# Two unused 32-byte tiles at the right end of SBUF are taken away in a fused attention and mixture-of-experts kernel

## The chip, the cores and the metric

The kernel runs on one core of one Trainium2 chip. The metric is the time of one execution in device microseconds (us); lower is better. TensorE (PE in the rows) multiplies, and its weight loads stand in rows of their own (PEld). VectorE is DVE, ScalarE is ACT, GpSimd is POOL, and SyncE (SP) issues the transfers. SBUF is the on-chip memory in which a tile takes the same byte range in each of 128 partitions; an address below is a byte offset within a partition.

## The reference

Attention over pooled keys and values, then a dense layer pair with a cosine gate, then eight experts whose outputs are mixed with a balanced gate. All inputs and outputs are float32.

```python
attn = softmax(q @ mean8(k).T / 8) @ mean8(v)         # 4 x 8 heads, 576 rows, 72 pooled columns
x = attn as [2304, 512]
h = x @ w_in;  x = (h * cos(h)) @ w_out               # 512 -> 2048 -> 512
P = exp(x @ w_gate - max);  8 rounds of row and column normalization   # [2304, 8]
for e in range(8):
    h = maximum(x @ w1[e], 0)                         # 512 -> 1024
    out += P[:, e:e+1] * (h @ w2[e])                  # 1024 -> 512
```

The eight experts take about three quarters of the time. The text calls `x @ w1[e]` the first layer and `h @ w2[e]` the second layer.

## The kernel before, in words

**Arithmetic.** A float32 operand is split into a high part rounded to the format fp32r and a low part that holds the rest (`whi`/`wlo` and `vhi`/`vlo` of the weights, `xc` of the activations, `gh`/`gl` of the inner results). A product is three fp32r matmuls: high by high, high by low, low by high. Both expert layers use Strassen's seven products P1 to P7 in the place of eight blocks.

**Work of one step.** The experts' inner width is cut into 16 units of 512 columns, and the rows into 3 pairs of 768. A step is one unit with one pair, so there are 48 steps. In a step the first layer (`first_layer`, L1077) issues 2 x 7 x 6 = 84 matmuls of 384 columns: the weights `whi`/`wlo` are loaded into the array and `xc` streams through it. The second layer (`strassen_layer`, L1451 to L1458) issues 3 x 7 x 6 = 126 matmuls of 256 columns. Here the inner results `gh`/`gl` are loaded into the array, and the weights `vhi`/`vlo` stream through it:

```python
for n, (l, m) in enumerate(((gh, w[name][0]), (gh, w[name][1]), (gl, w[name][0]))):
    nc.tensor.matmul(out=ps, lhsT=l[:, r], rhs=m[:, k], start=(start and h + n == 0),
                     stop=(h + n == 3), skip_group_check=True)
```

Each of these matmuls reads 256 values of 4 bytes (1,024 bytes) per partition from `vhi` or `vlo` as the streamed operand and 128 values (512 bytes) per partition from `gh` or `gl` as the loaded one. Over 48 steps that is 6,048 matmuls.

**Order of the work.** Every instruction is a node of a graph. `Graph.schedule` lists the nodes engine by engine by a simulated clock, with estimated durations and due times, and the order is then fixed. Waits follow from the tiles that two nodes share. The first-layer matmuls of one step are interleaved with the second-layer ones of the step before.

**Memory.** Tiles live in pools, and pools in groups. A group is opened at one side of SBUF (`left` from low addresses up, `right` from the highest address down). The groups on the right are these:

```python
early = g.group("early", "right")
mid = g.group("mid", "right", (early,))
ahead = g.group("ahead", "right", (early,), mid)
turn = g.group("turn", "right", (early,), ahead)
late = g.group("late", "right", (early, turn), ahead)
```

`early` serves the attention (`kbd`, `at`, `band`, `pt`, `qc`, and `cw`/`m` of the weight conversion). Once it is closed, `mid` takes its place at the right end, `ahead` (the second layer's weights, `k_w2`) lies below `mid`, and `late` (`sf`, `s5`, `c22`, `t5`: temporaries of VectorE and ScalarE) below that. `xc` in the first-layer ring, `whi`/`wlo`, `gh`/`gl` and the output sums are on the left.

Of the kernel before, what the change touches and what calls it, by code (L numbers as in the profile page):

```python
# [10 lines left out]
F32 = mybir.dt.float32  # L11
# [12 lines left out]
P = 128  # L24
# [53 lines left out]
class Group:  # L78
# [9 lines left out]
    def open(self):  # L88
        if self.stack is not None:
            return  # L90
        if self.over:
            self.over.open()
        for g in self.after:
            if not g.closed and g.stack is not None:
                g.stack.close()
            g.closed = True
        self.stack = self.graph.ctx.enter_context(ExitStack())
        if self.name in ("early", "mid"):
            edge = self.stack.enter_context(self.graph.tc.tile_pool(name="edge" + self.name, bufs=1, side=self.side))
            edge.tile([P, 8], F32, name="edge" + self.name)  # L100
        for pool in self.pools:
            self.pools[pool] = self.stack.enter_context(
                self.graph.tc.tile_pool(name=pool, bufs=1, side=self.side, reuse_waits="tile"))
# [1482 lines left out]
```

## Time and profile before

| what | value |
|---|---|
| median of 3 runs | 1929.78 us (1928.85 to 1931.67) |
| the profiled execution's own time | 1929.34 us |
| its span from first to last instruction | 1927.6 us |
| PE busy | 1907.3 us, 99% of the span |
| DVE, ACT, POOL busy | 79%, 57%, 22% of the span |
[...]

The profile was taken on one execution: its time is 1.7 us more than its span, which is launch and end. A matmul's duration in a row runs from its start to its last result, so that durations of neighbours overlap; the pace of a stream of matmuls is read from the starts of the first and a later one and the number between them.

### The profile page before, as it was taken

What the parts mean: (1) busy time and instruction counts of PE and PEld (TensorE: products, weight loads), DVE (VectorE), ACT (ScalarE), POOL (GpSimd) and SP (SyncE); (2) the same over time, 40 slices, a digit from 0 to 9 for tenths busy, and PEclk for the clock granted to TensorE, in tenths of its full rate; (3) what the DMA queues carried; (4) which work ended last, traced back from release to release, by engine and by line L of the source; (5) the groups of instructions that cost most, each with busy time, mean ns of one, the idle gap of its engine ahead of it and who ended that gap; (6) DMA issues with size and microseconds to landing.
All of it is one profiled execution on the core that took longest, in us unless ns stands there. A gap on an engine that the chain in (4) does not pass through costs nothing.

```text
span 1927.6 us, 34292 instructions
## 1 busy us (share of the span) xinstructions
PE 1907.3 (99%) x13012; PEld 1872.0 (97%) x13012; DVE 1531.9 (79%) x2823; ACT 1096.6 (57%) x2354; POOL 427.4 (22%) x341
## 2 busy tenths in 40 slices
PE   8999999999999999999999999999999999999999
PEld 6789998899999999999999999999999999999998
DVE  8998888987787777777787787777777877877776
ACT  5664445675556666555556565565555565655553
POOL 2523245453202021212112021212121120212120
PEclk9999999999999999999999999999999999999999
DMA  8567564487656546546546455465465464554552
GB/s 294 169 193 236 194 198 138 176 288 239 231 225 229 228 186 237 212 181 236 211 177 262 168 231 229 184 238 210 183 236 211 178 262 170 229 231 180 229 216 113
DMA packets 107478, 406.79 MB, mean 211 GB/s; under 512 B 11825, under 2 KB 16561, under 8 KB 107313
## 3 DMA queue, kind: packets, MB, share of 16 engines
q1 hardware_dynamic: 106768, 403.55, 56.4%
q8 instruction: 102, 1.67, 0.4%
q0 software_dynamic: 544, 1.05, 0.3%
q14 instruction: 64, 0.52, 0.1%
HBM read 363.40 MB, written 41.16 MB: 210 GB/s over the span
## 4 chain that ended last, share of the span: by engine, by line
PE 91%; DVE 5%; ACT 1%; DMA 1%; issue 1%; POOL 0%; SPq 0%; DVEq 0%; POOLq 0%; ACTq 0%
PE pc L1457 21%; PE py L1077 17%; PE qc L1457 16%; PE pv L1077 11%; PE px L1077 11%; PE po L894 3%; PE po L895 3%; PE po L896 3%; PE ph L894 1%; PE ph L896 1%; PE ph L895 1%; PE ptr L803 0%; DVE at L540 0%; DVE cw L858 0%; PE psc L714 0%
## 5 line engine op out<-in xcount | busy, mean ns | idle before, releaser
L1457 PE MATMUL pc<-vhi,gl 128*128 128x256 f32 x1152 | 321.6, 279 | 0.0
L1457 PE MATMUL pc<-vhi,gh 128*128 128x256 f32 x1152 | 321.5, 279 | 0.0
L1457 PE MATMUL pc<-vlo,gh 128*128 128x256 f32 x1152 | 321.3, 279 | 0.0
L1077 PE MATMUL py<-xc,whi 128*128 128x384 f32 x1152 | 293.3, 335 | 0.0
L540 POOL TENSOR_TENSOR raw<-raw 128x512 f32<-128x512 f32 x45 | 59.1, 1314 | 895.4 <-DVE wlo L540 542.1
L540 DVE TENSOR_TENSOR gl<-sf,gh 128x384 fp32r<-128x384 f32 x384 | 228.4, 624 | 30.9 <-ACT gh L523 30.9
L523 ACT ACTIVATE gh<-sf 128x384 fp32r<-128x384 f32 x384 | 195.0, 524 | 92.1 <-DVE sf L540 90.1
L1457 PE MATMUL qc<-vhi,gh 128*128 128x256 f32 x864 | 243.6, 282 | 0.9 <-DVE qc L540 0.5
L1457 PE MATMUL qc<-vhi,gl 128*128 128x256 f32 x864 | 241.6, 280 | 0.0
L1457 PE MATMUL qc<-vlo,gh 128*128 128x256 f32 x864 | 240.8, 279 | 0.0
L1457 PEld LDWEIGHTS pc<-vlo,gh 128*128 128x128 f32 x1152 | 216.6, 188 | 0.0
L1457 PEld LDWEIGHTS pc<-vhi,gl 128*128 128x128 f32 x1152 | 216.3, 188 | 0.0
L1457 PEld LDWEIGHTS pc<-vhi,gh 128*128 128x128 f32 x1152 | 215.5, 187 | 0.1
L1077 PEld LDWEIGHTS py<-xc,whi 128*128 128x128 f32 x1152 | 199.7, 188 | 1.3 <-ACT py L523 0.6
L1077 PE MATMUL px<-xc,whi 128*128 128x384 f32 x768 | 195.8, 335 | 0.0
L1077 PE MATMUL pv<-xc,whi 128*128 128x384 f32 x768 | 195.8, 335 | 0.0
L1077 PE MATMUL py<-xc,wlo 128*128 128x384 f32 x576 | 193.2, 335 | 0.0
L1457 PEld LDWEIGHTS qc<-vhi,gh 128*128 128x128 f32 x864 | 161.8, 187 | 3.4 <-DVE qc L540 1.1
L1457 PEld LDWEIGHTS qc<-vlo,gh 128*128 128x128 f32 x864 | 162.5, 188 | 0.0
L1457 PEld LDWEIGHTS qc<-vhi,gl 128*128 128x128 f32 x864 | 162.3, 188 | 0.0
L1077 PEld LDWEIGHTS pv<-xc,whi 128*128 128x128 f32 x768 | 130.7, 188 | 0.0
L1077 PEld LDWEIGHTS px<-xc,whi 128*128 128x128 f32 x768 | 130.5, 188 | 0.0
(235 smaller groups left out, 4676.1 us busy)
## 6 DMA issues: line engine op xcount, KB each, us to landing
xc<-xc SPq DMA_DIRECT2D x357, 768.0 KB, 6.7
wc<-wac SPq DMA_DIRECT2D x112, 256.0 KB, 3.3
raw<-wa SPq DMA_DIRECT2D x48, 512.0 KB, 4.0
raw<-wb SPq DMA_DIRECT2D x48, 512.0 KB, 7.4
wac<-wc SPq DMA_DIRECT2D x64, 256.0 KB, 3.8
out<-acc SPq DMA_DIRECT2D x18, 256.0 KB, 2.0
qc<-qt SPq DMA_DIRECT2D x30, 128.0 KB, 3.1
wf<-cw SPq DMA_DIRECT2D x12, 256.0 KB, 3.6
```

The costliest lines, as they stand in the source:

```text
L523: lambda: nc.scalar.activation(out=out(), in_=in_(), func=func, **{k: v() if callable(v) else v for k, v in more.items()}),
L540: (nc.gpsimd if e == "G" else nc.vector).tensor_tensor(out=out(), in0=in0(), in1=in1(), op=op)
L894: nc.tensor.matmul(out=ps, lhsT=lh, rhs=rh, start=(i == 0), stop=False)
L895: nc.tensor.matmul(out=ps, lhsT=lh, rhs=rl, start=False, stop=False)
L896: nc.tensor.matmul(out=ps, lhsT=ll, rhs=rh, start=False, stop=(i == total - 1))
L1077: nc.tensor.matmul(out=ps(), lhsT=l[:, k], rhs=r[:, c, :], start=(start and c + n == 0), stop=(c + n == 3), skip_group_check=True)
L1457: nc.tensor.matmul(out=ps, lhsT=l[:, r], rhs=m[:, k], start=(start and h + n == 0), stop=(h + n == 3), skip_group_check=True)
```

## The change

It takes away the code that puts a tile of 8 float32 values (32 bytes per partition) at the right end of SBUF when the groups `early` and `mid` open. Nothing reads or writes these tiles.

```diff
         self.stack = self.graph.ctx.enter_context(ExitStack())
-        if self.name in ("early", "mid"):
-            edge = self.stack.enter_context(self.graph.tc.tile_pool(name="edge" + self.name, bufs=1, side=self.side))
-            edge.tile([P, 8], F32, name="edge" + self.name)
         for pool in self.pools:
```

All other tiles keep their sizes and their order. The instructions of every engine stay the same 21,017 in the same order, with the same waits; only addresses differ. Every tile on the right lies 32 bytes higher, and no tile on the left moves. The addresses, as a remainder of division by 512 (all slices that a second-layer matmul reads of one operand share it):

| tiles | role | before | after |
|---|---|---|---|
| `vhi`, `vlo` (7 slots each) | second layer, streamed | 128 | 160 |
| `gh`, `gl` (18 slots each) | second layer, loaded | 320 | 320 |
| `whi`, `wlo` | first layer, loaded | 192 | 192 |
| `xc` in its ring of 7 | first layer, streamed | 192 | 192 |
| `t5`, `s5`, `c22`, `sf` | temporaries of DVE and ACT | 128 | 160 |
| `dhi`, `dlo` (dense layer's last third) | loaded | 128 or 448 | 160 or 480 |
| `kbd0` of batches 0 and 2 | attention scores, streamed | 32 | 64 |
| `kbd1` of batches 1 and 3 | attention scores, streamed | 320 | 352 |

So before, 128, 192 and 320 are all multiples of 64; after, the streamed operand of the second layer and the temporaries are at 32 past a multiple of 64. In the attention the two tiles change roles: before `kbd0` is at 32 past a multiple of 64 and `kbd1` at a multiple; after it is the other way round.

## Rows read from the trace of the kernel before

**Rows 1.** The page, part 1: busy time by engine.
```profile
PE 1907.3 (99%) x13012; PEld 1872.0 (97%) x13012; DVE 1531.9 (79%) x2823; ACT 1096.6 (57%) x2354; POOL 427.4 (22%) x341
```

**Rows 2.** Windows of the experts: length, each engine's busy time and instructions, clock, DMA.
```profile
600.00:1000.00 400.00, 400.00 (x2850) 399.51 (x2849) 308.88 (x565) 237.15 (x521) 67.39 (x49) 1.00 0.56 216
1000.00:1400.00 400.00, 400.00 (x2858) 399.52 (x2857) 308.75 (x563) 221.62 (x495) 65.39 (x48) 1.00 0.54 208
1400.00:1800.00 400.00, 400.00 (x2852) 399.40 (x2851) 311.36 (x567) 225.55 (x504) 70.07 (x51) 1.00 0.55 213
```

**Rows 3.** The page, part 4: the chain that ended last, by engine and line.
```profile
PE 91%; DVE 5%; ACT 1%; DMA 1%; issue 1%; POOL 0%; SPq 0%; DVEq 0%; POOLq 0%; ACTq 0%
PE pc L1457 21%; PE py L1077 17%; PE qc L1457 16%; PE pv L1077 11%; PE px L1077 11%; PE po L894 3%; PE po L895 3%; PE po L896 3%; PE ph L894 1%; PE ph L896 1%; PE ph L895 1%; PE ptr L803 0%; DVE at L540 0%; DVE cw L858 0%; PE psc L714 0%
```

**Rows 4.** Second layer's matmuls, groups by line: busy us, mean ns, idle before.
```profile
L1457 PE MATMUL pc<-vhi,gl 128*128 128x256 f32 x1152 | 321.6, 279 | 0.0
L1457 PE MATMUL pc<-vhi,gh 128*128 128x256 f32 x1152 | 321.5, 279 | 0.0
L1457 PE MATMUL pc<-vlo,gh 128*128 128x256 f32 x1152 | 321.3, 279 | 0.0
L1457 PE MATMUL qc<-vhi,gh 128*128 128x256 f32 x864 | 243.6, 282 | 0.9 <-DVE qc L540 0.5 <-DVE pc L540 0.3
L1457 PE MATMUL qc<-vhi,gl 128*128 128x256 f32 x864 | 241.6, 280 | 0.0
L1457 PE MATMUL qc<-vlo,gh 128*128 128x256 f32 x864 | 240.8, 279 | 0.0
```

**Rows 5.** Timeline of PE: start us, length us; the second row starts 66 matmuls later.
```profile
1907.14 0.28 PE L1457 MATMUL pc<-vhi,gh 128*128 128x256 f32 x1
...
1914.91 0.28 PE L1457 MATMUL qc<-vhi,gh 128*128 128x256 f32 x1
```

**Rows 6.** The windows of rows 2, second-layer matmuls (L1457) alone, then first-layer ones (L1077).
```profile
600.00:1000.00 400.00, 220.12 (x1698) 215.30 (x1698) 1.00 0.56 216
1000.00:1400.00 400.00, 222.62 (x1722) 217.89 (x1722) 1.00 0.54 208
1400.00:1800.00 400.00, 220.61 (x1704) 215.76 (x1704) 1.00 0.55 213
...
600.00:1000.00 400.00, 220.24 (x1152) 194.52 (x1151) 1.00 0.56 216
1000.00:1400.00 400.00, 217.09 (x1136) 191.79 (x1135) 1.00 0.54 208
1400.00:1800.00 400.00, 219.10 (x1148) 193.78 (x1147) 1.00 0.55 213
```

**Rows 7.** Score matmuls (L714), window 65 to 77, all streaming kbd1: ns min/median/max.
```profile
L714 PE MATMUL psc<-kbd,qc x20: 285/286/310, 65.3 to 76.8; 128*128 128x144 f32 x20
```

**Rows 8.** The same line, window 98 to 109, all streaming kbd0.
```profile
L714 PE MATMUL psc<-kbd,qc x20: 285/286/390, 99.0 to 108.6; 128*128 128x144 f32 x20
```

**Rows 9.** Timeline of PE, merged: four score matmul records on kbd1, then four on kbd0.
```profile
39.16 0.66 PE L714 MATMUL psc<-kbd,qc 128*128 128x144 f32 x4
...
108.27 0.65 PE L714 MATMUL psc<-kbd,qc 128*128 128x144 f32 x4
```

**Rows 10.** The attention's transposes (L803), whole span: ns min/median/max.
```profile
L803 PEld LDWEIGHTS ptr<-ident,at x144: 112/115/118, 17.3 to 359.8; 128*72 128x72 f32 x144
```

**Rows 11.** Who writes kbd, whole span: ns min/median/max.
```profile
L523 ACT ACTIVATE kbd<-ks x4: 427/435/443, 78.4 to 292.4; 64x288 f32<-64x288 f32 x4
L583 POOL MEMSET kbd<- x2: 578/580/583, 0.9 to 2.6; 128x576 f32 x2
```

## The prediction

> **What bounds the kernel now.** I read the page's busy times first. PE is busy for 99% of the span, and no other engine is above 79% [rows 1]. A share over the whole span can hide stages, so the windows of the experts come next: in three stretches of 400 us, PE's rows cover all 400.00 us at full granted clock, while DVE has about 91 us free in each and ACT more than 160 [rows 2]. The chain that ended last says the same in another way: 91% of it is PE, and the two expert lines make up 76% of the whole (L1457, second layer, 37%; L1077, first layer, 39%) [rows 3]. PE hardly ever waits there: before the 6,048 matmuls of the second layer it sat idle for 0.9 us in all [rows 4]. So this stage has one price, the time from one matmul's start to the next, and whatever the change adds to that is paid in full, once per matmul.
>
> That pace is not the duration in the groups (279 ns), because matmuls overlap. From the timeline, 66 second-layer matmuls take 1914.91 - 1907.14 = 7.77 us, so one takes 117.7 ns [rows 5]. The three windows hold 5,124 second-layer matmuls and 3,436 first-layer ones [rows 6]. The first kind takes 5,124 x 0.1177 = 603 us of the 1,200, which leaves 597 us for the second kind, or 173.7 ns each. From 256 columns to 384 the pace rises by 56.0 ns, so a column costs 0.4375 ns, and 117.7 - 256 x 0.4375 = 5.7 ns do not depend on columns. The second layer in all: 6,048 x 117.7 ns = 712 us, 37% of the span, as the chain says.
>
> **The change, part by part.** It removes no instruction and no wait, since nothing touches the two tiles. What it can change is how long an instruction takes to read or write at its new address.
>
> *Streamed weights of the second layer, 128 to 160.* This is the only term on the path. The trace of before holds no fp32r matmul that streams from an address at 32 past a multiple of 64, so its price is bounded from both sides. From below, without a gain: the score matmuls of the attention. Those of the window at 65 us stream `kbd1` (at a multiple of 64), those of the window at 98 us stream `kbd0` (32 past one), and the medians are 286 ns and 286 ns [rows 7, 8]. Four records in a row take 0.66 us on `kbd1` and 0.65 us on `kbd0` [rows 9]. So here the remainder costs nothing: 0 us. But these are float32 matmuls of 144 columns, and a record follows the one before after (0.65 - 0.286) / 3 = 0.121 us, or 0.84 ns per column, about half the column rate of the second layer. A read that is slightly longer could hide in that and not at 0.4375 ns per column.
>
> From above: if the memory gives a row of 1,024 bytes in pieces of 64, a row that starts at 128 is 16 pieces and one that starts at 160 is 17. The additional piece holds 32 wanted bytes at either end, which is 8 columns. If it costs no more than the columns whose place it takes, that is 8 x 0.4375 = 3.5 ns per matmul, or 21 us; if a whole piece of 16 columns is lost, 7.0 ns, or 42 us.
>
> That a piece is 64 bytes is an assumption; no row shows it. I take the middle between the score matmuls' 0 and the 3.5 ns of 8 columns, 1.75 ns, because the nearest rows show no cost at about half the rate: 6,048 x 1.75 ns = 10.6 us.
>
> [...]
>
> *Temporaries of DVE and ACT (`t5`, `s5`, `c22`, `sf`), and the writing of `vhi` and `vlo`.* I price these at nothing on the path. Where a row mixes both remainders, durations hardly spread: ACT's writes of `kbd` go to both tiles and take 427 to 443 ns, GpSimd's fills 578 and 583 [rows 11]. If DVE's and ACT's operations all took 5% more, DVE would need 15 us more of the 91 it has free per window [rows 2]. If that cover failed, the sum of `t5` into PSUM would come late first, since the next product group accumulates on it. PE would then idle before the `qc` matmuls, where the 0.9 us of today stand [rows 4].
>
> *Loaded operands that move (`dhi`, `dlo`, and `at` in the attention).* The four heads of `at` lie 288 bytes apart, so that they alternate between a multiple of 64 and 32 past one, before as after; their 144 weight loads take 112 to 118 ns [rows 10], so nothing hangs on it there. `dhi` and `dlo` are loaded 192 times in the dense layer, beside matmuls of 384 columns; even 3.5 ns for each would be 0.7 us. The attention's two `kbd` tiles change roles, which by rows 7 and 8 costs nothing. Transfers that move are a few queries and parked activations, and DMA is 1% of the chain [rows 3].
>
> **Sum.** The profiled execution took 1929.34 us. 1929.34 + 10.6 = 1939.9 us. The median of the runs lies 0.4 us above the profiled time, so I say 1940 us.
>
> **The rivals.**
>
> *No change.* Every row that shows both remainders shows equal times [rows 7 to 11], and PE reads the same bytes in the same order. Against it: none of those rows is an fp32r stream at the pace of 0.4375 ns per column. The time would be 1929.3 us, 1930 beside the median. [...]
>
> [...]
>
> *Slower through DVE.* The part on temporaries gives its price: nothing until DVE has lost its 91 us per window. I count it with the slower case.
>
> **How the numbers follow.** A measurement of this kernel tells a change from none at about 0.2%, which is 3.9 us or 0.64 ns per second-layer matmul. Slower through the streamed operand: 0.48. I put it first because this is the one stream that runs at the full column rate with no idle time behind it, so the cover that the score matmuls may have had is missing; that is a judgement, and the rows do not force it. No change: 0.30. Faster: 0.22. The slower case alone runs from 1933 to 1972 us (0.64 to 7.0 ns). For 8 times in 10 I cut both tails: at the top above 1965 (5.9 ns), which leaves out about 0.07, and at the bottom below 1914 (half of the per-column excess won back), which leaves out about 0.11.
>
> **What would show it.** In the timeline of after, the pace of an unbroken stretch of second-layer matmuls: 119.4 to 119.5 ns if I am right, 117.7 if nothing happens, 115 if the collision is won. The first layer must stay at 173.7 ns, since none of its operands move. The score matmuls on `kbd1`, now 32 past a multiple of 64, should stay at 286 ns. PE's idle time before the `qc` matmuls should stay near 1 us; if it grows to several us, DVE or ACT became slower and my path is wrong. I am wrong altogether if the first layer's pace moves too, or if the second layer's pace moves by more than 7 ns, which no count of pieces explains.

## The result and the profile after

The changed kernel takes 1941.12 us (median; 1939.68 to 1942.14) against 1929.55 us for the kernel before. The ratio is 1.0057, with a 95% interval of 1.0044 to 1.0069. The forecast was 1940 us, slower; the time and the place are right, and the reason that I gave for them is not, as the experiments show.

The page of the kernel after, part 1 (busy time by engine) and part 4 (the chain), has the shape of [rows 1, 3]. PE is 12.4 us busier, its weight loads (PEld) 13.5 us, and the other engines differ by less than 5 us:

```profile
PE 1919.7 (99%) x13012; PEld 1885.5 (97%) x13012; DVE 1536.6 (79%) x2823; ACT 1097.0 (57%) x2354; POOL 425.9 (22%) x341
...
PE 92%; DVE 5%; ACT 1%; issue 1%; DMA 0%; SPq 0%; DVEq 0%; ACTq 0%
```

The groups by line of the kernel after answer to [rows 4] (lines stand three lower, since three were taken away). No idle time has come in front of these matmuls (0.8 us in the place of 0.9), so that no engine has become late; the mean duration rose by 1 to 4 ns:

```profile
L1454 PE MATMUL pc<-vhi,gl 128*128 128x256 f32 x1152 | 325.5, 283 | 0.0
L1454 PE MATMUL pc<-vlo,gh 128*128 128x256 f32 x1152 | 325.4, 282 | 0.0
L1454 PE MATMUL pc<-vhi,gh 128*128 128x256 f32 x1152 | 323.3, 281 | 0.0
...
L1454 PE MATMUL qc<-vhi,gh 128*128 128x256 f32 x864 | 244.8, 283 | 0.8 <-DVE qc L537 0.5 <-DVE pc L537 0.3
L1454 PE MATMUL qc<-vhi,gl 128*128 128x256 f32 x864 | 244.0, 282 | 0.0
L1454 PE MATMUL qc<-vlo,gh 128*128 128x256 f32 x864 | 242.9, 281 | 0.0
```

The timeline of PE in the kernel after, at the same place of the program as [rows 5] (the second row again starts 66 matmuls later):

```profile
1917.83 0.28 PE L1454 MATMUL pc<-vhi,gh 128*128 128x256 f32 x1
...
1925.75 0.28 PE L1454 MATMUL qc<-vhi,gh 128*128 128x256 f32 x1
```

66 matmuls take 7.92 us in the place of 7.77, so one takes 120.0 ns in the place of 117.7. The windows of the kernel after answer to [rows 2], whole first, then the second layer's and the first layer's matmuls alone as in [rows 6]:

```profile
600.00:1000.00 400.00, 400.00 (x2827) 399.71 (x2826) 307.50 (x559) 235.72 (x516) 67.31 (x49) 1.00 0.56 214
1000.00:1400.00 400.00, 400.00 (x2835) 399.71 (x2834) 309.65 (x563) 222.15 (x494) 65.28 (x48) 1.00 0.54 207
1400.00:1800.00 400.00, 400.00 (x2827) 399.63 (x2825) 309.47 (x560) 222.09 (x495) 69.97 (x51) 1.00 0.55 212
...
600.00:1000.00 400.00, 221.84 (x1686) 216.25 (x1684) 1.00 0.56 214
1000.00:1400.00 400.00, 224.57 (x1712) 219.43 (x1713) 1.00 0.54 207
1400.00:1800.00 400.00, 221.86 (x1687) 216.26 (x1685) 1.00 0.55 212
...
600.00:1000.00 400.00, 217.99 (x1141) 193.90 (x1142) 1.00 0.56 214
1000.00:1400.00 400.00, 214.61 (x1123) 190.45 (x1121) 1.00 0.54 207
1400.00:1800.00 400.00, 217.70 (x1140) 193.74 (x1140) 1.00 0.55 212
```

The three windows hold 8,489 matmuls where they held 8,560. The 48 steps are 10,080 matmuls, so they take 10,080 x 1200 / 8,489 = 1424.9 us in the place of 1413.1: 11.8 us more, which is the whole loss. By the working of the prediction, 5,085 second-layer matmuls at 120.0 ns leave (1200 - 610.2) / 3,404 = 173.3 ns for the first layer, which was 173.7. The starts of the matmuls say the same: within first-layer runs they follow each other after 173.8 ns on average, which was 174.0. The loss lies in the second layer alone. The granted clock is 1.00 as before.

### The profile page after: what moved, and what is told of

Its sections match the earlier page's. It is cut to its first block, busy times and chain, and to the rows that moved or that the text cites. A ratio compares the mean times of both kernels' runs of the same rounds, so it can differ in the third digit from the quotient of the medians.

```text
span 1938.6 us, 34292 instructions
## 1 busy us (share of the span) xinstructions
PE 1919.7 (99%) x13012; PEld 1885.5 (97%) x13012; DVE 1536.6 (79%) x2823; ACT 1097.0 (57%) x2354; POOL 425.9 (22%) x341
## 4 chain that ended last, share of the span: by engine, by line
PE 92%; DVE 5%; ACT 1%; issue 1%; DMA 0%; SPq 0%; DVEq 0%; ACTq 0%
PE pc L1454 21%; PE py L1074 17%; PE qc L1454 16%; PE pv L1074 11%; PE px L1074 11%; PE po L891 3%; PE po L892 3%; PE po L893 3%; PE ph L891 2%; PE ph L893 2%; PE ph L892 2%; DVE m L851 0%; DVE cw L855 0%; PE ptr L800 0%; PE px L814 0%
## 5 line engine op out<-in xcount | busy, mean ns | idle before, releaser
L1454 PE MATMUL pc<-vhi,gl 128*128 128x256 f32 x1152 | 325.5, 283 | 0.0
L1454 PE MATMUL pc<-vlo,gh 128*128 128x256 f32 x1152 | 325.4, 282 | 0.0
```

## The experiments

The prediction's theory is called the piece theory in the expectations: the streamed row starts at 32 past a multiple of 64 and costs one more piece. Its first rival is the distance theory, which grew out of the case "faster" of the prediction: what counts is the address of the loaded operand (`gh`, `gl`) less that of the streamed one (`vhi`, `vlo`). The distance was 320 - 128 = 192 bytes and became 160. The second rival, the temporaries theory, blames the tiles of ScalarE and VectorE that moved too.

All kernels compute the whole reference with the same instructions in the same order; only addresses differ. Distances below are remainders of division by 512.

### Which of the moved tiles counts

*weights_only* puts one tile of 32 bytes above the temporaries in the place of the two at the right end, so that the weights stay at 160 and the temporaries return to 128. *temps_only* is the kernel before with this third tile: weights at 128, temporaries at 96.

```diff
-        if self.name in ("early", "mid"):
+        for n in {'late': (8,)}.get(self.name, ()):
...
-            edge.tile([P, 8], F32, name="edge" + self.name)
+            edge.tile([P, n], F32, name="edge" + self.name)
```

That is the edit of weights_only against the kernel before; temps_only has `{'early': (8,), 'mid': (8,), 'late': (8,)}` there.

> Streamed weights of the second layer at 160, loaded inner results at 320, as after the change, but the temporaries t5, s5, c22, sf back at 128. Piece theory (the streamed row starts at 32 past a multiple of 64) and distance theory (what counts is the loaded operand's address less the streamed one's, 160 in the place of 192): both 1941 us, a mean pace of 119.6 ns in the second layer. Temporaries theory (ScalarE and VectorE are slowed at 160 and hold TensorE up): 1929.5 us, 117.8 ns.

> Streamed weights at 128 and inner results at 320, as before the change, and the temporaries alone at 96, which is 32 past a multiple of 64. Piece and distance theory: 1929.5 us, pace 117.8 ns. Temporaries theory: 1941 us.

Measured: weights_only 1940.76 us, ratio to the kernel before 1.0055 (1.0038 to 1.0072); temps_only 1928.70 us, 0.9995 (0.9983 to 1.0007). The timeline of weights_only at the same place as before:

```profile
1917.74 0.28 PE L1457 MATMUL pc<-vhi,gh 128*128 128x256 f32 x1
...
1925.66 0.28 PE L1457 MATMUL qc<-vhi,gh 128*128 128x256 f32 x1
```

That is 7.92 us for 66, or 120.0 ns, with the temporaries back in their old place. The temporaries theory falls. Of the tiles that moved here, the weights are the only ones that the expert steps' matmuls read, and they carry the whole change.

### Which address counts: the streamed one or both

*inner_with* has no tile at the right end (weights at 160) and moves the inner results by 32 as well, to 352. *inner_alone* keeps the two tiles (weights at 128) and moves the inner results to 352. The pad lies on the left ahead of the first pool of `gh`; what lies above it on the left (the dense layer's operands and temporaries, two output sums) moves with it.

```diff
         for pool in self.pools:
+            if pool in {'gph': 8}:
...
+                pad.tile([P, {'gph': 8}[pool]], F32, name="pad" + pool)
```

> Without the two tiles, so that the weights are streamed from 160, and the inner results moved by 32 as well, to 352: the distance is 192 again. Piece theory: the streamed row still starts at 32 past a multiple of 64, so a pace of 119.6 ns in the expert steps or more; 1941 to 1945 us, the upper end since the dense layer's inner results are streamed, from 352 too. Distance theory: 117.8 ns, 1929.5 us.

> With the two tiles, weights streamed from 128, inner results loaded from 352: distance 224. Piece theory: streamed rows start at a multiple of 64, pace 117.8 ns in the expert steps, 1929.5 to 1934 us (the dense layer streams inner results from 352). Distance theory: 224 is as far from 192 as 160 is, so a pace clearly above 117.8 ns, about 119.6, and 1941 us.

Measured: inner_with 1931.86 us, 1.0011 (0.9998 to 1.0023); inner_alone 1936.99 us, 1.0036 (1.0024 to 1.0049). The timeline of inner_with at the same place:

```profile
1908.11 0.28 PE L1460 MATMUL pc<-vhi,gh 128*128 128x256 f32 x1
...
1915.88 0.28 PE L1460 MATMUL qc<-vhi,gh 128*128 128x256 f32 x1
```

The weights are streamed from 160, as in the kernel after, and the pace is 7.77 us for 66, or 117.7 ns, as in the kernel before. Of the two operands of these matmuls only the loaded one was moved against the kernel after, and that gave the pace back. The piece theory falls here, since it puts the cost on the streamed row alone.

inner_alone is half a miss for the distance theory too: its long run has the pace of before (1914.80 to 1922.57 us, 117.7 ns), while the kernel is slower by 0.36%. In 600 to 1800 us it issues 8,507 matmuls, against 8,556 before. So a distance of 224 (117.7 ns) is not as bad as 160 (120.0 ns) inside the long run. What is lost is lost in the shorter runs, and not in one place: by the table of means below, a second-layer matmul takes 0.5 ns more there, the last one before a first-layer matmul 5.4 ns more, and a first-layer matmul 0.6 ns more, although no operand of the first layer moved.

### The distance, step by step

Eight kernels differ from the one before by the size of the two tiles alone. First came 64, 96, 256 and 352 bytes, then 128, 160, 192 and 224. Each byte more at the right end lowers the streamed address and so makes the distance greater by one.

```diff
-        if self.name in ("early", "mid"):
+        for n in {'early': (40,), 'mid': (40,)}.get(self.name, ()):
...
-            edge.tile([P, 8], F32, name="edge" + self.name)
+            edge.tile([P, n], F32, name="edge" + self.name)
```

That is edge160. The two numbers are the bytes in the kernel's name divided by 4. The temporaries move along with the weights; temps_only shows them to cost nothing at 96 (1928.70 us, ratio 0.9995), and no run shows them alone at the other places.

> Tiles of 64 bytes in the place of 32: weights streamed from 96 (32 past a multiple of 64), inner results loaded from 320, distance 224. Piece theory, already in trouble: 1941 us, mean pace 119.8 ns within second-layer runs. Pair theory (what counts is the distance of the two addresses, with 160 bad, 192 and 224 good): 118.2 ns and 1931 to 1937 us, as when 224 was made by moving the inner results.

> Tiles of 96 bytes: weights streamed from 64, inner results loaded from 320, distance 256. Piece theory: 64 is a multiple of 64, so 1929.5 us and 117.8 ns. Pair theory says nothing sure of a distance not yet run; if bad distances are narrow, 1929.5 us.

> Tiles of 256 bytes: weights streamed from 416 past a multiple of 512 (32 past one of 64), inner results from 320, distance 416, which is 160 plus 256. Piece theory: 1941 us, 119.8 ns. If the distance counts with a period of 256 bytes: the same 119.8 ns; with a period of 512 this is a new distance and may be anything from 117.8 ns up.

> Tiles of 352 bytes, the largest that fit: weights streamed from 320 and inner results loaded from 320, distance 0. Piece theory: a multiple of 64, so 1929.5 us and 117.8 ns. If equal addresses collide all along a row, well above: 122 ns or more and 1955 us.

> Tiles of 128 bytes: weights streamed from 32, inner results from 320, distance 288. If the pace repeats with the distance every 128 bytes, 288 is 160 again: mean pace 119.8 ns within second-layer runs, the same uneven row of six spacings, 1941 us. If it repeats only every 256 bytes, 288 is 32, which has not been run: anything from 116.7 to 120 ns.

> Tiles of 160 bytes: weights streamed from 0, inner results from 320, distance 320. Repeats every 128: 320 is 192 again, as before the change: 117.8 ns, 1928 us. Repeats every 256 only: 64, not run, 116.7 to 120 ns.

> Tiles of 192 bytes: weights streamed from 480 past a multiple of 512 (32 past one of 64), inner results from 320, distance 352. Repeats every 128: 352 is 224 again: 116.7 ns, 1926.5 us, the fastest of all, although the streamed row starts at 32 past a multiple of 64. Repeats every 256 only: 96, not run.

> Tiles of 224 bytes: weights streamed from 448, inner results from 320, distance 384. Repeats every 128: 384 is 256 and 0 again: 119.7 ns, 1941 us, although the streamed row starts at a multiple of 64. Repeats every 256 only: 128, not run.

Measured; the pace is read from the start of the last long run of second-layer matmuls and the start of the 66th after it, and "matmuls" are PE's in the window from 600 to 1800 us:

| kernel | streamed, loaded | distance | starts, us | pace, ns | matmuls | ratio to before (interval) |
|---|---|---|---|---|---|---|
| edge352 | 320, 320 | 0 | 1920.33, 1928.24 | 119.8 | 8,482 | 1.0076 (1.0054 to 1.0099) |
| after | 160, 320 | 160 | 1917.83, 1925.75 | 120.0 | 8,484 | 1.0057 (1.0044 to 1.0069) |
| before | 128, 320 | 192 | 1907.14, 1914.91 | 117.7 | 8,556 | 1 |
| inner_with | 160, 352 | 192 | 1908.11, 1915.88 | 117.7 | 8,539 | 1.0011 (0.9998 to 1.0023) |
| edge64 | 96, 320 | 224 | 1905.08, 1912.78 | 116.7 | 8,572 | 0.9993 (0.9982 to 1.0004) |
| inner_alone | 128, 352 | 224 | 1914.80, 1922.57 | 117.7 | 8,507 | 1.0036 (1.0024 to 1.0049) |
| edge96 | 64, 320 | 256 | 1919.20, 1927.12 | 120.0 | 8,482 | 1.0070 (1.0047 to 1.0093) |
| edge128 | 32, 320 | 288 | 1910.95, 1918.76 | 118.3 | 8,520 | 1.0028 (1.0019 to 1.0038) |
| edge160 | 0, 320 | 320 | 1889.40, 1896.89 | 113.5 | 8,661 | 0.9903 (0.9886 to 0.9919) |
| edge192 | 480, 320 | 352 | 1917.77, 1925.60 | 118.6 | 8,480 | 1.0054 (1.0039 to 1.0069) |
| edge224 | 448, 320 | 384 | 1915.90, 1923.73 | 118.6 | 8,501 | 1.0046 (1.0031 to 1.0061) |
| edge256 | 416, 320 | 416 | 1918.32, 1926.24 | 120.0 | 8,481 | 1.0073 (1.0050 to 1.0095) |

The two ends of the table as rows of the timeline, edge96 first:

```profile
1919.20 0.28 PE L1457 MATMUL pc<-vhi,gh 128*128 128x256 f32 x1
...
1927.12 0.28 PE L1457 MATMUL qc<-vhi,gh 128*128 128x256 f32 x1
```

and edge160:

```profile
1889.40 0.28 PE L1457 MATMUL pc<-vhi,gh 128*128 128x256 f32 x1
...
1896.89 0.28 PE L1457 MATMUL qc<-vhi,gh 128*128 128x256 f32 x1
```

The long run is only one place. The second table has means over all starts from 600 to 1800 us: the time from one second-layer matmul to the next, from the last of a run to the first-layer matmul behind it, and from one first-layer matmul to the next.

| kernel | second to second, ns | second to first, ns | first to first, ns |
|---|---|---|---|
| before | 118.0 | 114.3 | 174.0 |
| after | 119.6 | 123.1 | 173.8 |
| inner_with | 118.3 | 117.4 | 173.8 |
| inner_alone | 118.5 | 119.7 | 174.6 |
| edge160 | 115.2 | 113.6 | 173.9 |
| edge192 | 118.9 | 118.8 | 175.5 |

So about three tenths of what the change costs is paid at the ends of second-layer runs, where the next weights to be loaded are those of the first layer: 365 times 8.8 ns is 3.2 us, beside 4,714 times 1.6 ns, 7.5 us, inside the runs.

Three things follow. First, alignment of the streamed row to 64 bytes is neither needed nor enough: edge64 streams from 96 and is as fast as the kernel before (0.9993 of its time, 116.7 ns beside 117.7), edge96 streams from 64 and is as slow as the kernel after (1.0070 beside 1.0057, 120.0 ns both).

Second, the two pairs of distances that lie 256 bytes apart, 160 with 416 and 256 with 0, give equal paces (120.0 and 120.0; 120.0 and 119.8) and nearly equal counts. Even the row of single spacings is the same: from the fifth matmul of the long run on, after and edge256 both repeat 117, 125, 116, 123, 119 and 120 ns, while edge96 and edge352 keep to 119 to 121 ns. In the ten kernels with the loaded operand at 320, however, the distance can't be told from the streamed address alone; that the loaded one counts rests on inner_with and inner_alone. A repeat every 128 bytes, which I had expected for the last four runs, is refuted: 32, 64, 96 and 128 past a multiple of 256 give 118.3, 113.5, 118.6 and 118.6 ns, where 160, 192, 224 and 0 gave 120.0, 117.7, 116.7 and 120.0. So edge192, which I had put down as the fastest, is slower than the kernel before by 0.54%.

Third, one distance stands out, 64 past a multiple of 256. edge160 was expected at 117.8 ns with a repeat every 128 bytes and at 116.7 to 120 ns without one; at 113.5 ns it missed both. Three other expectations missed as well: edge64 came in at 1926.49 us where the pair theory had 1931 to 1937, edge96 at 1941.39 us where both theories leaned to 1929.5, and edge352 at 119.8 ns, between the piece theory's 117.8 and the 122 or more that I had put down as a guess for two equal addresses.

edge160 beats both kernels: 1910.96 us, 1.0% less than the kernel before. Its windows, whole, show where that comes from: PE covers every window as before, with more matmuls in each, and DVE still has about 86 us free in each:

```profile
600.00:1000.00 400.00, 400.00 (x2889) 399.16 (x2888) 311.84 (x572) 239.24 (x527) 68.30 (x49) 1.00 0.56 216
1000.00:1400.00 400.00, 400.00 (x2887) 399.21 (x2886) 314.38 (x571) 226.58 (x506) 74.20 (x54) 1.00 0.56 219
1400.00:1800.00 400.00, 400.00 (x2890) 399.01 (x2889) 313.77 (x575) 224.69 (x504) 65.49 (x48) 1.00 0.54 209
```

## Why the prediction was right or wrong, point by point

**What bounds the kernel: right.** PE's pace in the experts was the only price. It rose by 2.3 ns in a long run (117.7 to 120.0). The 48 steps took 11.8 us more and the span 11.0 us (1927.6 to 1938.6), so that the rest of the program was slightly faster. The first layer's pace stayed at 174 ns (174.0 before, 173.8 after), as the prediction said it must.

**The size of the term: nearly right, by luck.** I took 1.75 ns per second-layer matmul, between 0 and 3.5; it is 2.3 ns in the long run and 11.8 us / 6,048 = 1.95 ns over all steps. The sum of 1940 us is 1.1 us short of the median.

**The reason for the term: wrong.** The step that failed is "if the memory gives a row of 1,024 bytes in pieces of 64, a row that starts at 128 is 16 pieces and one that starts at 160 is 17". No run shows such pieces, nor the 3.5 ns that the 1.75 ns is half of: inner_with streams from 160 at 117.7 ns and edge96 from 64 at 120.0 ns. What they show in its place is that the pace goes with the place of both operands: with the weights streamed from 160 it is 120.0 ns beside inner results at 320 and 117.7 ns beside inner results at 352. The score matmuls, which I had set aside as too slow a stream, were a correct hint that 32 past a multiple of 64 costs nothing by itself (286 ns on either tile; edge64, streaming from 96, has 116.7 ns). In the kernel after `kbd1` is at 32 past a multiple of 64, and its window shows what the prediction said it would:

```profile
L711 PE MATMUL psc<-kbd,qc x17: 283/286/293, 65.8 to 76.9; 128*128 128x144 f32 x17
```

**The case "faster": the right quantity with the wrong sign.** What stood behind its 0.22 was a guess of mine: that the reads of the two operands meet, so that their place relative to each other counts, and that 160 in the place of 192 might make this cheaper. No run shows that the reads meet, nor the per-column excess from which the prediction's 1914 us and 115 ns come. What the runs show in its place are the paces at the two distances, 117.7 ns at 192 and 120.0 ns at 160. The place of the operands relative to each other does count: with the streamed address at 160 throughout, moving the loaded operand by 32 bytes took the pace from 120.0 to 117.7 ns, and with the streamed address at 128 the same move left it at 117.7 ns (long runs). So for these fp32r matmuls, what one operand's address costs depends on the other's. But 160 is one of the worst places, and what can be won lies elsewhere, at 320: 117.7 - 113.5 = 4.2 ns in the long run, and 118.0 - 115.2 = 2.8 ns on average inside the runs of the expert steps.

**Temporaries, roles of `kbd`, loaded operands of the dense layer: nothing, as priced.** weights_only and temps_only show the first, for temporaries at 96, 128 and 160 (1940.76 us at 128 beside 1941.12 at 160; 0.9995 of the time before at 96); PE's idle time before the `qc` matmuls is 0.8 us against 0.9. The score matmuls take 286 ns in the median on either tile, before and after, and a load of `dhi` or `dlo` 188 ns in the median before and after. The tile of `early` alone was not run.

**What stays open.** Why the distance counts is not shown. The distance is not the whole law either: 224 made in two ways gives 116.7 and 117.7 ns. And edge192 loses more than its long run says: 118.6 ns there, yet as few matmuls in 1,200 us (8,480) as kernels at 120.0. By the table of means, 4.6 us of its loss between 600 and 1800 us lies inside first-layer runs (3,037 times 1.5 ns), although both operands of the first layer stay at 192. Its six groups of first-layer matmuls last 336 to 339 ns on average in that window where the kernel before has 335 to 336, without idle time; one of them, before and in edge192:

```profile
L1077 PE MATMUL px<-xc,wlo 128*128 128x384 f32 x327 | 109.6, 335 | 0.0
...
L1077 PE MATMUL px<-xc,wlo 128*128 128x384 f32 x324 | 109.8, 339 | 0.0
```

So the pace of these matmuls is not set by their own two addresses alone: at the same two it is 174.0 ns before and 175.5 ns in edge192. Whether the second-layer run ahead of it or the temporaries, which moved along, are the reason, no run separates.

## What to carry to other kernels

In this kernel, with TensorE busy for 99% of the span, the price of a matmul was the distance of starts in an unbroken run, and with the same instructions in the same order addresses alone took that price from 113.5 to 120.0 ns. Read the pace from the timeline for each kind of matmul, in short runs as well as in a long one, and try some unused bytes between the streamed and the loaded operand: here 160 bytes in the place of 32 gave 1.0%. An address effect should be tested by moving the other operand too; moving one alone, as this change did, can't tell alignment from distance.

## What the runs showed of the hardware that was not expected

For fp32r matmuls with 256 streamed columns and 128 loaded ones, the pace in long runs went from 113.5 to 120.0 ns with nothing but the operands' addresses, 5.7%. It repeated for the two pairs of distances that differ by 256 bytes (120.0 and 120.0, 120.0 and 119.8 ns). At the first layer's shape (384 columns, both operands at 192) the pace stayed at 174 ns in the kernels before and after, but it was 175.5 ns on average in edge192, where only other tiles had moved.
